# Delta-rule attention and two MoE layers on one core: both row halves in one product, joined grams, anchored filler, later weights

## The chip, the cores and the metric

One core of a Trainium2 chip runs the whole program. The metric is the device time of one execution in microseconds; the median of three runs is given. Smaller is better.

## The reference

For 32 heads of 768 steps, width 48, an attention with a matrix state is computed; its output (3072 tokens of 384) goes through a gated layer and then through a second layer with a leaky nonlinearity:

```python
k_n = k / (norm(k) + 1e-6)
for t in range(S):
    y[:, :, t] = q_t @ state
    state = state + beta_t * outer(k_t, v_t - k_t @ state)
x = ((x @ w_a) * (x @ w_b)) @ w_out
h = x @ w_in
out = (maximum(h, 0) + alpha * minimum(h, 0)) @ w_out2
```

## The kernel before

The 768 steps are cut into 6 superchunks (c) of two steps (j = 0, 1) of 64 positions; in one step 32 pairs of batch and head are worked on, 16 in each row half of the partitions (x = 0, 1). For one superchunk the keys are multiplied with themselves (`g`, the grams of keys, into `ef`) and with the queries (`g` again, into Z[:, 1] and Z[:, 2]); keys lie in Z[:, 0], rows 64 to 111 for one half and 0 to 47 for the other. The 64x64 triangular system of each pair is solved by blocks of 32: `inverting` (line 760) inverts the two diagonal blocks of all pairs at once on VectorE, 31 steps of a multiply into `itmp` and an add into `inv`, a PSUM tile that the code calls `eu`. Then the off-diagonal block is two products, `w` and `xx`; in the first superchunk `first_sides` (861) does them, later ones use `diagonal` and `offdiag`. `w` reads `hw` (the transposed inverse) and `ef`; its result is copied into the upper rows of `hw`; `xx` reads that and `TT`, and its result is copied into `TT`, whose lower column half is a copy of the upper one with zeros above.

`step` (889) then runs for each j: `rp` (old state times keys, not in the very first step), `v` minus it on VectorE, `up` (TT times v) copied to `SU`, `sp` (keys times that) subtracted into the next state, and `yp` (queries times state and `SU`), which is the attention output. `columns` (1108) splits yp into a rounded part on ScalarE and a rest on VectorE, the tile `x` that the first layer reads. That layer streams `p` (two products of x with w_a and w_b, nine instructions of 512 columns each) and `o`, twelve blocks m for each superchunk; the second layer's products are `h` and `o`. Its first superchunk runs from the end of the first attention superchunk on; the second superchunk's attention is interleaved with it.

Weights arrive packed (`raw`), and are decoded by two ScalarE operations, a VectorE shift and a GpSimd add into `W`, then split into `wu` by ScalarE and GpSimd (`decode`, 1020, and `prepare`, 1093). The first four of the twelve have rooms from the start; the later eight use the rooms rawd, rawb, rawc and rawe in turn (1373). `behind` (1039) holds the operation after whose start their transfers are put on SP's queue: the load of the values v of the second superchunk.

The order on each engine is not written by hand. All operations are recorded first; `Schedule.run` (353) then plays them through with a cost for each (`costs`, 277), a level of urgency (`rec.urgent`, added to it) and a model of the product clock, of instruction fetch and of the transfers, and the order that comes out is emitted through one line (203), which is why every row of the profile names L203. An operation recorded on `nc.evict` may go to ScalarE or VectorE, one on `nc.split` to GpSimd or VectorE, as the planner finds it. TensorE's gaps before the first large product are filled with `spin` products of a zero tile `still`: up to 200 are recorded (1238), and the planner puts them into the gaps that it foresees, from the clearing of `still` on:

```python
at = max(free[e], end[warm] if end[warm] else 1e9)
while True:
    each = SPIN if fast(at) else 2 * SPIN
    if at + each > b - REST - 0.08 * (b - free[e]) or len(spins) == len(s.spins):
        break
    spins.append(at)
```

VectorE clears the rooms of two Z and of TT at the start (583, 597). For the second superchunk (N) the grams of keys and of queries are separate products (1290 to 1293), emptied by ScalarE.

## Time and profile before

| | |
|---|---|
| runs | 1018.55 us median of 3 (1017.36 to 1018.96) |
| profiled execution | 1014.57 us, span 1012.8 us |
| TensorE | 996.3 us busy (98% of the span), mean granted clock 0.993 |
| VectorE, ScalarE, GpSimd | 619.2, 459.9 and 486.8 us busy |
| chain that ended last | TensorE 92%, VectorE 5% |
| transfers | 61.41 MB |

The profile is one execution on the chip. A row of the timeline gives a start and a length, merged where an engine repeats the same operation (the count follows the x), then in brackets the idle time of the engine just before and what ended it. TensorE's products have ends that are modelled, so a busy TensorE is not always one at its best. Tiles bear the names that the code gives them: the inverse of the first superchunk is `inv`.

### The profile page before, as it was taken

What the parts mean: (1) busy time and instruction counts of PE and PEld (TensorE: products, weight loads), DVE (VectorE), ACT (ScalarE), POOL (GpSimd) and SP (SyncE); (2) the same over time, 40 slices, a digit from 0 to 9 for tenths busy, and PEclk for the clock granted to TensorE, in tenths of its full rate; (3) what the DMA queues carried; (4) which work ended last, traced back from release to release, by engine and by line L of the source; (5) the groups of instructions that cost most, each with busy time, mean ns of one, the idle gap of its engine ahead of it and who ended that gap; (6) DMA issues with size and microseconds to landing.
All of it is one profiled execution on the core that took longest, in us unless ns stands there. A gap on an engine that the chain in (4) does not pass through costs nothing.

```text
span 1012.8 us, 23700 instructions
## 1 busy us (share of the span) xinstructions
PE 996.3 (98%) x10047; PEld 816.4 (81%) x10047; DVE 619.2 (61%) x1229; ACT 459.9 (45%) x846; POOL 486.8 (48%) x395
## 2 busy tenths in 40 slices
PE   7989999999999999999999999999999999999997
PEld 6777877888888788888878888888888888888886
DVE  7789868846794687568667689343343343433333
ACT  5836785464546454645588786121121221211211
POOL 5467955634653366346456986333333333333332
PEclk8899999999999999999999999999999999999999
DMA  9436433002200220000025542010010020000000
GB/s 236 174 99 226 149 81 94 19 2 66 95 1 22 69 72 1 18 19 32 16 82 173 162 145 84 1 31 32 1 63 1 1 63 1 32 0 1 32 1 32
DMA packets 27083, 61.41 MB, mean 61 GB/s; under 512 B 4320, under 2 KB 8928, under 8 KB 26976
## 3 DMA queue, kind: packets, MB, share of 16 engines
q1 hardware_dynamic: 26544, 59.50, 19.1%
q8 instruction: 79, 1.29, 0.5%
q10 hardware_dynamic: 432, 0.39, 0.1%
q14 instruction: 28, 0.23, 0.1%
HBM read 50.44 MB, written 9.44 MB: 59 GB/s over the span
## 4 chain that ended last, share of the span: by engine, by line
PE 92%; DVE 5%; issue 1%; ACT 1%; DMA 1%; SPq 0%; POOL 0%; DVEq 0%; ACTq 0%
PE o L203 33%; PE p L203 27%; PE h L203 19%; PE g L203 3%; PE spin L203 2%; PE yp L203 2%; PE up L203 2%; DVE inv L203 1%; PE sp L203 1%; DVE itmp L203 1%; PE rp L203 1%; PE xx L203 1%; PE w L203 1%; DMA raw<-in_w_o_dram 1%; DVE a L203 0%
## 5 line engine op out<-in xcount | busy, mean ns | idle before, releaser
L203 PE MATMUL p<-x,wu 128*128 128x512 f32 x1296 | 318.3, 394 | 0.9 <-DVE x L203 0.4
L203 PEld LDWEIGHTS p<-x,wu 128*128 128x128 f32 x1296 | 240.3, 188 | 54.5 <-issue 2.8
L203 POOL TENSOR_TENSOR g<-neg,g 128x512 fp32r<-128x512 f32 x95 | 124.2, 1308 | 259.6 <-ACT g L203 257.1
L203 POOL TENSOR_TENSOR wu<-W,wu 128x768 fp32r<-128x768 f32 (+1 forms) x122 | 175.4, 1442 | 141.6 <-ACT wu L203 141.5
L203 PE MATMUL o<-g,v 128*128 128x512 f32 x870 | 211.4, 388 | 0.0
L203 PE MATMUL h<-x,v 128*128 128x512 f32 x864 | 211.3, 389 | 0.0
L203 DVE TENSOR_SCALAR neg<-h,al 128x512 f32<-128x512 f32 (+1 forms) x97 | 72.2, 745 | 225.6 <-PE h L203 225.6
L203 ACT CAST g<-neg 128x512 fp32r<-128x512 f32 (+1 forms) x97 | 59.7, 616 | 300.5 <-DVE neg L203 278.4
L203 PEld LDWEIGHTS o<-g,v 128*128 128x128 f32 x870 | 162.5, 188 | 33.5 <-POOL g L203 0.2
L203 PEld LDWEIGHTS h<-x,v 128*128 128x128 f32 x864 | 162.2, 188 | 33.7 <-DVE neg L203 0.2
L203 PE MATMUL o<-g,wu 128*128 128x512 f32 x648 | 164.6, 394 | 1.1 <-ACT g L203 1.0
L203 PEld LDWEIGHTS o<-g,wu 128*128 128x128 f32 x648 | 120.1, 188 | 28.0 <-ACT g L203 1.8
L203 ACT CAST wu<-W 128x768 fp32r<-128x768 f32 (+1 forms) x144 | 97.1, 676 | 83.6 <-PE p L203 61.7
L203 POOL TENSOR_TENSOR g<-a,g 128x512 fp32r<-128x512 f32 x50 | 67.7, 1355 | 52.3 <-ACT g L203 51.9
L203 DVE TENSOR_TENSOR inv<-inv,itmp 128x110 f32<-128x110 f32 (+12 forms) x256 | 75.1, 293 | 8.7 <-ACT eu L203 0.4
L203 DVE SCALAR_TENSOR_TENSOR neg<-h,neg 128x512 f32<-128x512 f32 (+1 forms) x97 | 66.5, 686 | 3.3
L203 PE MATMUL g<-Z 48*64 48x64 f32 (+1 forms) x1024 | 63.7, 264 | 4.4 <-issue 2.0
L203 ACT COPY a<-p 128x512 f32<-128x512 f32 x72 | 42.2, 587 | 49.2 <-PE p L203 34.6
L203 DVE TENSOR_TENSOR a<-p,a 128x512 f32<-128x512 f32 x59 | 40.5, 687 | 32.1 <-PE p L203 28.5
L203 PEld LDWEIGHTS g<-Z 48*64 48x64 f32 x1024 | 47.4, 149 | 7.8 <-issue 2.7
L203 DVE TENSOR_TENSOR itmp<-inv,gd 128x96 f32<-128x96 f32 (+8 forms) x150 | 40.7, 271 | 10.5 <-ACT gd L203 6.1
L203 ACT CAST g<-a 128x512 fp32r<-128x512 f32 x59 | 36.5, 619 | 22.7 <-DVE a L203 22.4
(107 smaller groups left out, 950.6 us busy)
## 6 DMA issues: line engine op xcount, KB each, us to landing
v<-in_w_o_dram SPq DMA_DIRECT2D x16, 384.0 KB, 3.4
v<-in_w_in_dram SPq DMA_DIRECT2D x16, 384.0 KB, 3.5
Z<-in_kt_dram SPq DMA_DIRECT2D x24, 192.0 KB, 3.4
Z<-in_qt_dram SPq DMA_DIRECT2D x24, 192.0 KB, 3.8
v<-in_vn_dram SPq DMA_DIRECT2D x12, 384.0 KB, 3.3
x2d<-x2s SPq DMA_DIRECT2D x18, 256.0 KB, 2.3
xf<-x2d SPq DMA_DIRECT2D x18, 256.0 KB, 2.7
raw<-in_w_a_dram SPq DMA_DIRECT2D x11, 384.0 KB, 7.0
```

Of the source, the lines that this page charges most:

```text
L203: getattr(s.engines[op.eng], name)(*(real(x) for x in op.a), **{w: real(x) for w, x in op.k.items()})
```

## The change

1. In `first_sides` w and xx become products over all 128 rows: a tile `both` with zeros holds the two row halves in separate columns, so one product with 64 columns does both. For this `hw` is transposed into TT's lower column half, copied into `both` (ScalarE for one half, GpSimd for the other), and TT's upper half is copied there between w and xx; TT's zeros and the copy of its lower half are written after that, all on GpSimd. Left operands get zeros (`got`, `ef`). w and xx are recorded by j.
2. Keys come in one transfer of 128 rows, padded with zeros on the host, in place of two of 48 rows.
3. The second superchunk's grams of keys and queries are one product with 128 columns (`pair`), emptied by `nc.evict`; so are the copies to SU of the first superchunk, `keep` in `mate`, and one of the first key evictions goes to VectorE.
4. The beta multiply of the first inversion is split between VectorE (8 of 32 columns) and GpSimd; the clears of Z go to GpSimd.
5. Spins come in two sets of 150; the second hangs on a ScalarE operation that reads row 20 of the inverse and writes into `still`.
6. The transfers of the later weights are put behind the last product of the step (`yp`), rawd takes the room of `both`, and in the second step the state update is less urgent than yp. yp of the second step has banks of its own.
7. `rp` runs half by half in the first superchunk, and rp and yp can be cut into pieces (`cut`) between which the planner may put other products. The cost of a transfer goes by its rows.

Left out below are the emission of `neg`, the bookkeeping of the marks, the clears that move and the host's padding.

```diff
@@ -282,7 +287,7 @@
...
-            t.cost, t.lag = 0.42 if t.eng == SP_ else 0.1, 0.05 + n / (9.8e4 if name == "raw" else 6.5e4)
+            t.cost, t.lag = 0.42 if t.eng == SP_ else 0.1, 0.05 + n / (9.8e4 if moved.p[1] - moved.p[0] > 64 else 5.2e4)
@@ -412,17 +417,21 @@
...
-                    at = max(free[e], end[warm] if end[warm] else 1e9)
-                    while True:
+                    first = chunk["at"] == 2 * len(spins)
+                    mark = anchor if end[anchor] else warm
+                    at = max(free[e], end[mark])
+                    while end[mark] and len(spins) < (len(s.spins) if end[anchor] else s.early):
...
-                        if at + each > b - REST - 0.08 * (b - free[e]) or len(spins) == len(s.spins):
+                        if at + each > b - (0 if first else REST if end[anchor] else REST + 0.08 * (b - free[e])):
...
+                        if end[anchor] and len(spins) < s.early:
+                            spins += [None] * (s.early - len(spins))
...
-                        spins.append(None)
+                        spins += [None] * (len(s.spins) + 1 - len(spins))
@@ -622,8 +629,7 @@
...
-            nc.sync.dma_start(Z[64:112, 0], s.kt[c, j, 0])
-            nc.sync.dma_start(Z[0:48, 0], s.kt[c, j, 1])
+            nc.sync.dma_start(Z[:, 0], s.kt[c, j])
@@ -710,7 +716,7 @@
...
-                nc.vector.tensor_scalar(L["ef"][:, j * 16 + i4 : j * 16 + i4 + 4, :], g[:, :, 0, :], -1.0, None, ALU.mult)
+                nc.evict.neg(L["ef"][:, j * 16 + i4 : j * 16 + i4 + 4, :], g[:, :, 0, :])
@@ -723,6 +729,20 @@
...
+    def pair(s, L, j, i4, tag):
+
+        nc, Z = s.nc, L["Z"][j]
+        g = s.bank("g", tag).rearrange("p (i w n) -> p i w n", w=2, n=64)
+        for i in range(4):
+            for x, rows, both in ((0, slice(64, 112), slice(0, 2)), (1, slice(0, 48), slice(0, 3, 2))):
+                nc.tensor.matmul(
+                    g[64 * x : 64 * x + 64, i], Z[rows, 0, i4 + i, :], Z[rows, both, i4 + i, :], start=True, stop=True,
+                )
+        nc.evict.neg(L["ef"][:, j * 16 + i4 : j * 16 + i4 + 4, :], g[:, :, 0, :])
+        for x in range(2):
+            sl = slice(64 * x, 64 * x + 64)
+            nc.evict.neg(Z[sl, 1 + x, i4 : i4 + 4, :], g[sl, :, 1, :])
+
@@ -734,7 +754,7 @@
...
-        s.nc.scalar.activation(L["ef"][:, j * 16 + i8 : j * 16 + i8 + 8, :], g, AF.Copy, scale=-1.0)
+        (s.nc.vector if L.get("first") and j and i8 else s.nc.scalar).neg(L["ef"][:, j * 16 + i8 : j * 16 + i8 + 8, :], g)
@@ -766,13 +786,14 @@
...
-        nc.vector.tensor_tensor(a0[:, :, 0:8], a0[:, :, 0:8], bt[:, :, 0:8], ALU.mult)
-        nc.vector.tensor_tensor(a0[:, :, 8:32], a0[:, :, 8:32], bt[:, :, 8:32], ALU.mult)
+        bt = L["bt"].unsqueeze(1).to_broadcast([128, 32, 32])
+        for eng, ms in ((nc.vector, slice(0, 8)), (nc.gpsimd, slice(8, 32))):
+            eng.tensor_tensor(a0[:, ms], a0[:, ms], bt[:, ms], ALU.mult)
...
-            column = a0[:, k:32, m : m + 1].to_broadcast([128, nt, k])
+            column = a0[:, m, k:32].unsqueeze(2).to_broadcast([128, nt, k])
@@ -858,33 +879,54 @@
...
-    def first_sides(s, L):
-
-        nc, ef, hw, eu = s.nc, L["ef"], s.ap.tile([128, 32, 32], F32, tag="mb", name="hw", bufs=1), L["eu"]
+    def first_sides(s, L, both):
+
+        nc, ef, eu = s.nc, L["ef"], L["eu"]
+        got = s.ap.tile([128, 32, 32], F32, tag="mb", name="hw", bufs=1)
...
+        cols = (slice(0, 32), slice(32, 64))
+        urgent, s.nc.urgent = s.nc.urgent, 0.0
+        nc.gpsimd.memset(got, 0.0)
+        nc.gpsimd.memset(both, 0.0)
+        for x in range(2):
+            nc.gpsimd.memset(ef[high[x], :, 32:64], 0.0)
+        s.nc.urgent = urgent
+        hw = TT[:, :, 0:32]
...
+        for j in range(2):
+            js = slice(16 * j, 16 * j + 16)
+            for x in range(2):
+                (nc.gpsimd.tensor_copy if x else nc.scalar.copy)(both[low[x], js, cols[x]], hw[low[x], js])
...
-        for j in range(2):
-            for sl in low:
-                nc.gpsimd.tensor_copy(TT[sl, 16 * j : 16 * j + 16, 0:32], TT[sl, 16 * j : 16 * j + 16, 32:64])
-        stages = (
-            (low, ef[:, :, 32:64], hw, high, hw, [s.bank("w") for _ in range(2)]),
-            (high, hw, TT[:, :, 32:64], low, TT[:, :, 32:64], [s.bank("xx", "ab") for _ in range(2)]),
-        )
-        for here, left, right, there, to, banks in stages:
+
+        def side(left, there, to, bank):
+            bank = bank.rearrange("p (i n) -> p i n", n=64)
...
-                        for x in range(2):
-                            nc.tensor.matmul(
-                                banks[x][32 * q : 32 * q + 32, 32 * i : 32 * i + 32],
-                                left[here[x], 8 * q + i, :], right[here[x], 8 * q + i, :], start=True, stop=True,
-                            )
+                        nc.tensor.matmul(
+                            bank[32 * q : 32 * q + 32, i], left[:, 8 * q + i, :], both[:, 8 * q + i, :], start=True, stop=True,
+                        )
+                yield
...
-                        got = banks[x][32 * q : 32 * q + 32, 0:256].rearrange("p (i n) -> p i n", n=32)
-                        (nc.vector if x else nc.scalar).copy(to[there[x], 8 * q : 8 * q + 8, :], got)
+                        (nc.vector if x else nc.scalar).copy(to[there[x], 8 * q : 8 * q + 8, :], bank[32 * q : 32 * q + 32, :, cols[x]])
+
+        w = side(ef[:, :, 32:64], high, got, s.bank("w"))
+        next(w)
+        for j in range(2):
+            js = slice(16 * j, 16 * j + 16)
+            for _ in zip(range(1), w):
+                pass
+            for x in range(2):
+                (nc.gpsimd.tensor_copy if x else nc.scalar.copy)(both[high[x], js, cols[x]], TT[high[x], js, 32:64])
+        for sl in low:
+            nc.gpsimd.tensor_copy(TT[sl, :, 0:32], TT[sl, :, 32:64])
+        for sl in high:
+            nc.gpsimd.memset(TT[sl, :, 0:32], 0.0)
+        for _ in side(got, low, TT[:, :, 32:64], s.bank("xx", "ab")):
+            pass
@@ -910,12 +952,15 @@
...
-            for i in range(8):
-                for h, (o, _) in enumerate(halves):
-                    near, far = slice(64 * h, 64 * h + 64), slice(64 - 64 * h, 128 - 64 * h)
-                    nc.tensor.matmul(rp[h][near, i, :], Z[64:112, 0, o + i, :], SU[0][64:112, o + i, 0:48], start=True, stop=True)
-                    nc.tensor.matmul(rp[h][far, i, :], Z[0:48, 0, o + i, :], SU[1][0:48, o + i, 0:48], start=True, stop=True)
-                beside(i)
+            for i, h in [(i, h) for i in range(8) for h in range(2)] if c else [(i, h) for h in range(2) for i in range(8)]:
+                o = halves[h][0]
+                s.nc.now_tag = "cut" if i == 0 and not c else None
+                near, far = slice(64 * h, 64 * h + 64), slice(64 - 64 * h, 128 - 64 * h)
+                nc.tensor.matmul(rp[h][near, i, :], Z[64:112, 0, o + i, :], SU[0][64:112, o + i, 0:48], start=True, stop=True)
+                s.nc.now_tag = None
+                nc.tensor.matmul(rp[h][far, i, :], Z[0:48, 0, o + i, :], SU[1][0:48, o + i, 0:48], start=True, stop=True)
+                if h:
+                    beside(i)
@@ -938,7 +983,7 @@
...
-                    (nc.scalar if c or not x else nc.vector).copy(SU[x][64 * x : 64 * x + 64, hs, 0:48], ups[n][at : at + 64])
+                    (nc.scalar if c else nc.evict).copy(SU[x][64 * x : 64 * x + 64, hs, 0:48], ups[n][at : at + 64])
@@ -964,11 +1009,16 @@
...
-        yp = [s.bank("yp", tag) for _ in range(2)]
+        if st == 1:
+            yp = s.pools["g"].tile([128, 2, 512], F32, tag="inv", name="yp")
+            yp = [yp[:, n] for n in range(2)]
+        else:
+            yp = [s.bank("yp", tag) for _ in range(2)]
...
+                s.nc.now_tag = None if c else "cut"
@@ -978,6 +1028,7 @@
...
+                        s.nc.now_tag = None
@@ -1232,12 +1283,18 @@
...
+        rec.now_tag = "mark"
...
-        rec.now_tag, spin = "spin", A.bank("spin", "g")
-        for _ in range(200):
-            nc.tensor.matmul(spin, still[:, 0:128], still, start=True, stop=True)
-        rec.now_tag = None
+        spin = A.bank("spin", "g")
+
+        def spinning(n):
+            rec.now_tag = "spin"
+            for _ in range(n):
+                nc.tensor.matmul(spin, still[:, 0:128], still, start=True, stop=True)
+            rec.now_tag = None
+
+        spinning(150)
@@ -1270,7 +1327,7 @@
...
-        rawa, rawb, rawd = triple(wp, "w6"), triple(wp, "w7"), triple(xp, "x1")
+        rawa, rawb = triple(wp, "w6"), triple(wp, "w7")
@@ -1279,7 +1336,7 @@
...
-                A.fold(L, j, nc.gpsimd.tensor_copy)
+                A.fold(L, j, nc.vector.tensor_copy if j else nc.gpsimd.tensor_copy)
@@ -1287,15 +1344,16 @@
...
-        for n, (j, i8) in enumerate(HALF):
-            A.keep_keys(N, j, i8, A.gram_keys(N, j, i8, ("chain", "pre")[n % 2]))
-        for n, (j, i8) in enumerate(HALF):
-            A.keep_queries(N, j, i8, A.gram_queries(N, j, i8, ("chain", "pre")[n % 2]))
+        for n, (j, i4) in enumerate((j, i4) for j in range(2) for i4 in range(0, 16, 4)):
+            A.pair(N, j, i4, ("chain", "pre", "chain")[n % 3])
...
+        rec.now_tag = "mark"
+        nc.scalar.mul(still[:, 0:8], L["eu"][:, 20, 0:8], 0.0)
+        spinning(150)
@@ -1350,7 +1408,7 @@
...
-        A.first_sides(L)
+        A.first_sides(L, xp.tile([128, 32, 64], F32, tag="x1", name="both"))
@@ -1360,14 +1418,17 @@
...
-                    behind[:] = [A.load_values(1, N)]
+                    A.load_values(1, N)
+                    rec.urgent = URGENT * (j == 0)
+                if (i, j) == (5, 1):
...
+            behind[:] = [rec.ops[-1]]
...
-        rawc = triple(wp, "w8")
+        rawc, rawd = triple(wp, "w8"), triple(xp, "x1")
```

## Rows read from the trace of the kernel before

**Rows 1.** Stretches: busy time (and instructions) of each engine, granted clock, transfers

```profile
0.00:74.80 74.80, 65.28 (x1442) 54.14 (x1442) 60.54 (x133) 45.16 (x80) 40.47 (x55) 0.91 0.58 166
...
180.00:1012.80 832.80, 827.10 (x7220) 679.76 (x7218) 471.85 (x897) 342.76 (x646) 375.79 (x293) 1.00 0.13 41
```

**Rows 2.** Timeline of the start: start, length, engine, operation

```profile
0.80 1.83 POOL L203 MEMSET Z<- 32x1024 f32 x2 [0.29 <-POOLq L1587]
...
2.84 0.91 DVE L203 MEMSET Z<- 32x1024 f32 x1 [0.25 <-issue]
...
7.07 1.82 DVE L203 TENSOR_REDUCE ss<-sq 128x16 f32<-128x768 f32 x2
...
9.74 1.94 PEld L203 LDWEIGHTS g<-Z 48*64 48x64 f32 x62 [0.23 <-DMA Z<-in_kt_dram]
...
13.89 1.97 DVE L203 STREAM_TRANSPOSE eu<-ef 128x1024 f32<-128x1024 f32 x1 [2.37 <-POOL ef L203]
...
15.90 1.29 DVE L203 TENSOR_TENSOR eu<-eu,bt 128x256 f32<-128x256 f32 x2
...
17.11 0.19 DVE L203 TENSOR_TENSOR itmp<-inv,eu 128x31 f32<-128x31 f32 x1
...
30.29 1.47 POOL L203 TENSOR_TENSOR v<-v,m 128x768 f32<-128x768 f32 x1
```

**Rows 3.** Timeline, the end of the inversion and w

```profile
39.18 8.46 PE L203 MATMUL spin<-still 128*128 128x512 f32 x36
...
40.65 2.16 DVE L203 STREAM_TRANSPOSE hw<-inv 128x1024 f32<-128x1024 f32 x1
...
44.77 2.59 POOL L203 COPY TT<-TT 32x512 f32<-32x512 f32 x4 [3.44 <-DVE TT L203]
...
47.57 1.29 PE L203 MATMUL w<-hw,ef 32*32 32x32 f32 x128
```

**Rows 4.** Timeline, the two steps of the first superchunk

```profile
54.71 1.65 PE L203 MATMUL up<-v,TT 64*64 64x48 f32 x49 [1.06 <-issue]
...
57.26 1.03 DVE L203 COPY SU<-up 64x384 f32<-64x384 f32 x2
...
59.69 2.00 PE L203 MATMUL yp<-Z,SU 112*32 112x64 f32 x128
...
65.28 1.69 DVE L203 TENSOR_TENSOR v<-rp,v 128x384 f32<-128x384 f32 x3
```

**Rows 5.** Timeline, from the second yp to the first large product

```profile
69.02 1.31 SPq L203 DMA_DIRECT2D raw<-in_w_a_dram  x1
...
69.91 2.06 PE L203 MATMUL yp<-Z,SU 112*32 112x64 f32 x128
...
71.89 0.92 ACT L203 CAST x<-yp 128x256 fp32r<-128x256 f32 x3 [1.48 <-PE yp L203]
...
73.88 1.09 DVE L203 TENSOR_TENSOR x<-yp,x 128x256 fp32r<-128x256 f32 x3
...
74.78 4.35 PE L203 MATMUL p<-x,wu 128*128 128x512 f32 x18 [0.36 <-DVE x L203]
...
77.62 1.24 ACT L203 ACTIVATE W<-raw 128x1152 int32<-128x1152 uint32 x1 [4.81 <-DMA raw<-in_w_o_dram]
```

**Rows 6.** Stretches: the inversion, then up to the second one's start and end

```profile
17.11:40.62 23.51, 22.37 (x329) 19.07 (x329) 21.41 (x63) 16.60 (x27) 11.41 (x15) 0.71 0.85 294
...
40.62:70.89 30.27, 27.04 (x795) 22.12 (x798) 23.43 (x38) 17.47 (x34) 15.21 (x16) 1.00 0.13 34
...
70.89:118.60 47.71, 47.06 (x300) 37.79 (x289) 44.09 (x118) 30.96 (x44) 38.32 (x23) 1.00 0.64 209
```

**Rows 7.** Timeline, the end of the second superchunk's attention

```profile
157.08 0.96 ACT L203 COPY SU<-up 64x384 f32<-64x384 f32 x2 [0.25 <-PE up L203]
...
164.92 2.00 PE L203 MATMUL yp<-Z,SU 112*32 112x64 f32 x128
...
169.03 4.24 PE L203 MATMUL p<-x,wu 128*128 128x512 f32 x18
```

More of the change, by code (lines that the diff above doesn't have):

```diff
@@ L249, in __init__ @@
         s.spins = [op for op in rec.ops if op.tag == "spin"]
+        s.marks = [op for op in rec.ops if op.tag == "mark"]
+        s.early = sum(op.n < s.marks[1].n for op in s.spins)
         for op in rec.ops:
@@ L253, in __init__ @@
             t = s.tasks[-1] if s.tasks else None
-            if op.eng == PE_ and not large(op) and t and t.eng == PE_ and not t.large and t.ops[-1].n == op.n - 1:
+            if op.eng == PE_ and not large(op) and t and t.eng == PE_ and not t.large and t.ops[-1].n == op.n - 1 and op.tag != "cut":
                 t.ops.append(op)
@@ L363, in run @@
         clock = {"w": 0, "fast": False}
-        warm = s.of[min(s.spins[0].before)]
+        warm, anchor = (s.of[x.n] for x in s.marks)
         def fast(b):
@@ L1542, in columns, with stacked @@
         return a.reshape(NSC, 2, 2, D, 16, 64)
+    def stacked(a):
+        a = columns(a)
+        gap = np.zeros((NSC, 2, 16, 16, 64), a.dtype)
+        return np.concatenate([a[:, :, 1], gap, a[:, :, 0], gap], 2)
     def rows(a):
```

13 lines of the change are left out of this document (7 added, 6 removed).

## The prediction

> **What bounds the kernel now.** I read the stretches first. From the first large product to the end TensorE is nearly full: from 180 us on it is busy 827.10 of 832.80 us [rows 1]. Nothing in the change touches those products, so what it can give lies in the opening stretch, 74.8 us long, in which TensorE's 65.28 busy us are largely filler products on a tile of zeros (the "spins") and small products that wait for other engines. The forecast is therefore the answer to one question: how much earlier does the first large product (p, at 74.78 us) begin, and how much of that do the next 100 us keep?
>
> Second, the timeline of the start. VectorE clears rooms, sums squares from 7.07 us, transposes at 13.89 us after a wait of 2.37 us for GpSimd's fold, multiplies by beta for 1.29 us and begins the triangular inversion at 17.11 us [rows 2]. That inversion is one chain on one engine until 40.6 us, when its result is transposed into hw (40.65 plus 2.16, so 42.81 us). Now the first surprise: w, which needs only hw and old data, starts at 47.57 us, because TensorE works off 36 spins from 39.18 to 47.64 us [rows 3]. The order of every engine is written out ahead by a planner; between 17.11 and 40.62 us TensorE was granted a mean clock of 0.71, so a good part of that stretch ran at the 1.2 GHz level [rows 6], it came out behind the planner's clock, and the spins that were to fill a gap now stand in front of w.
>
> Third, the line from w to p: one product kind after another, each with a copy between [rows 4], and at its end p waits for VectorE's last splits of x at 73.88 us although ScalarE had its own done at 72.81 us [rows 5].
>
> **The change, part by part.** All sums are in the profiled execution (1014.57 us, span 1012.8 us and 1.8 us around it). It lies 4.0 us under the median of the runs shown; I take the difference off the median.
>
> (A) Start of the inversion. The beta multiply was 1024 elements in 1.29 us on VectorE; now GpSimd does 768 of them. VectorE keeps a quarter of the elements, with its fixed part some 0.4 us, so 0.9 us go. GpSimd's nearest row, 768 elements, takes 1.47 us [rows 2]; its columns are first read in the ninth of 31 steps, which lies about 4 us in (31 steps take 23.5 us), so the cover is wide; without it 1.1 us would come back. Four clears of 0.91 us leave VectorE (two for Z go to GpSimd at 0.92 each, two for TT go later): the sums at 7.07 us can begin when the squares are there. The fourth key eviction and one fold move to VectorE, so that GpSimd's fold no longer ends last. The keys come as one transfer of 512 KB for each j in place of two of 192 KB; the last landed at 9.74 us. No row has that form: if bytes rule it lands half a us later, if the number of transfers rules 1.5 us earlier. Together these three are worth between -0.5 and 2.4 us (the wait on the fold); with late keys as likely as early ones I take the middle, 1.2. Part A: 2.1 (0.4 to 3.3).
>
> (B) The spins. 42.81 to 47.57 is 4.76 us of pure delay. In the new kernel the second set of spins hangs on a ScalarE operation that reads row 20 of the inversion, so the planner's error counts only from there on, not from the start. Against it, w now needs hw copied into a tile with zeros: one 32x512 copy for each row half, GpSimd's row gives 0.65 (2.59 for four) [rows 3], and with hand-overs I count 1.25. Part B: 3.5 (0 if the spins end as late as now; 3.9 at best).
>
> (C) w and xx. From w to the end of the first up is 47.57 to 56.36, 8.79 us [rows 3, 4]. Each of w and xx becomes 32 products over all 128 rows with 64 columns in place of 64 products of 32 rows with 32 columns. The nearest row is yp: 64 products of 112 rows and 64 columns in 2.00 us, so 32 in 1.0 against 1.29 now, 0.6 saved on both. Between w and xx there is a new copy of TT into the tile (0.65, ScalarE and GpSimd beside each other), since that room is read by w first. The longest line is GpSimd's: four copies of 0.65, the two TT copies that were 2.59 as four, and two clears of 0.92 that were at the start [rows 2, 3], together 7.0 us in order from 42.81, and up reads all of it. So up begins about 7.5 us after hw and ends some 2 us later, against 13.55 now; with the 4.76 less 1.25 of part B this leaves 0.5. Pipelining w and xx by j adds a little: I take 0.8 (-3 if the copies line up one behind another, 3 if GpSimd's line is not the last).
>
> *A rule against this part.* w as 64 tiled products takes 1.29 us, and yp, which already runs over 112 rows, is no slower for each product [rows 3, 4]. The Trainium skill (TensorEngine Tiling (Array Packing), When to Use Tiling) says that a contraction of 32 rows should take fourfold row tiling, which is what the change gives up: four tiles in place of sixteen, half as many products, twice the columns, so up to four times the time. By it the sum would lose twice 3.9 us. yp's row speaks for my value.
>
> (D) The two steps, end of the first up (56.36) to the end of the second yp (71.97): 15.61 us. Three losses are visible [rows 4]: the SU copies wait for VectorE until 57.26 (0.9; now either engine may take them); the first yp, 2.00 us, stands between sp and rp (now it may be cut and passed); v is subtracted from 65.28 on, 3.6 us after yp ends, where rp needs about 1.1 and a hand-over (some 2 lost to other VectorE work, and that work stays). 4.9 at most, nothing at least; about half, 2.5, since VectorE has the same work in less time.
>
> (E) yp to p, 71.97 to 74.78. The second yp gets banks of its own, so p no longer waits for VectorE to empty two banks (73.88 plus 1.09), only for ScalarE's three casts, done at 72.81 [rows 5]. That is 2.0; the last products of the first nine still need VectorE's part 1.4 us later. I take 1.5 (0 to 2.4).
>
> Sum: 2.1 + 3.5 + 0.8 + 2.5 + 1.5 = 10.4 us, p at about 64.4.
>
> (F) What is given back. The weights after the fourth are now sent behind the second yp and not behind the last load of v: 69.02 us is 5.8 before p, the new place about 3.0, so they land 2.8 later against p. ScalarE already stood 4.81 us before the first of them (77.62) with a<-p queued behind it [rows 5], and TensorE's next p waits for that copy: 0.7 (0 to 2.8). VectorE is idle 6.84 us between 40.62 and 70.89 and 3.62 us up to 118.60 [rows 6]: the second inversion can come forward by A and most of the 6.84, some 8 us, so 2.4 less than p. The second superchunk has room for it: its last SU is done at 158.04 and yp issues at 164.92, 6.9 us later, with p at 169.03 [rows 7]. I count 0.5 (0 to 3). The padded keys add 128 KB a transfer in stretches where no row shows an engine waiting for keys: 0, up to 0.5. The joined grams of the second superchunk halve TensorE's products there; spins fill whatever that frees, so 0, as long as the evictions (24 small ones for 12) stay off VectorE's inversion. Net 10.4 - 1.2 = **9.2 us**: 1018.55 - 9.2 = 1009.3.
>
> **Rivals.**
> 1. *VectorE becomes the bound (0.14).* p moves but the second inversion does not, the second superchunk's x is late, TensorE stands near 165 us, and only A and some idle time count: 4 us, 1014.5. For it: 44.09 busy of 47.71 us [rows 6]. Against: the 6.9 us of room [rows 7].
> 2. *The 128-row products are slow (0.04).* If w and xx cost four times their rows, twice 3.9 us go: 9.2 - 7.8 = 1.4, 1017.1. yp's row speaks against it [rows 4]; this is the tiling rule of the Trainium skill's page named above.
> 3. *Most terms near their upper ends (0.12).* 15 us, 1003.5.
> 4. *The change doesn't do what it says (0.06).* All orders come from one planner whose transfer costs changed too. A new plan may put other work in each gap: 1018.5.
> 5. *Slower: transfers too late (0.14).* One room (rawd) takes four of the eight late weights, each after the last was decoded, and it now starts behind the tile of the first sides. If in each of the four turns ScalarE's wait grows by those 2.8 us and all of that, with the 0.7 of today's, reaches TensorE through the a<-p behind it, 14 us go against a gain of 9.9 (9.2 and the 0.7 already taken off): 4.1 slower, 1022.7. It decides as soon as the wait at 77.62 grows beyond 7 us in every turn. Against: today's wait costs TensorE under 1 us.
>
> **How the numbers follow.** The forecast (6 to 13 us, 1005.5 to 1012.5) has 0.50. Faster takes the forecast, rivals 1 and 3, and a third of rival 2: 0.77. Same (within 0.2%, about 2 us, which is what a measurement of this kernel can tell from no change) takes the rest of 2 and rival 4: 0.09. Slower is rival 5: 0.14. The range reaches from all terms at their upper ends (17 us, rounded to 1002) to no change at all (1018.5), and leaves out rival 5 and the tail of 3, under 2 in 10.
>
> **What would show it.** Right: the inversion begins near 15.0; w within 2 us of hw; up about 8 us after hw; p starting on ScalarE's x, near 64; after that stretches as full as before. Wrong: spins still in front of w (B), GpSimd's line of copies ending long before up or far later (C), p still on VectorE's x (E), or idle time of TensorE between p and 180 us with raw transfers or DVE as releaser (F, rivals 1 and 5).

## The result, and the profile after

The changed kernel takes 1025.05 us (median of 4 runs, 1023.73 to 1025.96) against 1018.75 us before: ratio 1.0063, 95% interval 1.0046 to 1.0081. It is slower by more than the 0.2% that can be told from no change; the forecast was 1009.3 us.

The profiled execution took 1023.73 us (span 1021.7). It lies 1.3 us under its median and that of before 4.2 under its own, so the two traces are 9.2 us apart where the medians are 6.3 apart. The stretches answer to [rows 1, 6]: the time up to p, the inversion, from its end to the start of the second superchunk's, and from there to the transpose of the second hw. Columns: busy us (and instructions) of PE, PEld, DVE, ACT, POOL; granted clock, DMA share, GB/s.

```profile
0.00:74.52 74.52, 62.09 (x1126) 51.89 (x1127) 53.01 (x116) 48.38 (x98) 47.17 (x61) 0.88 0.58 175
16.38:45.66 29.28, 27.16 (x264) 23.15 (x264) 21.41 (x62) 22.08 (x45) 16.32 (x25) 0.77 0.73 241
45.66:75.78 30.12, 25.00 (x692) 20.83 (x691) 23.56 (x39) 18.40 (x40) 18.86 (x20) 0.92 0.27 88
75.78:120.92 45.14, 44.57 (x218) 35.84 (x218) 40.22 (x110) 30.78 (x43) 37.95 (x22) 0.98 0.57 184
...
180.00:1021.70 841.70, 835.24 (x7251) 686.11 (x7250) 465.65 (x881) 357.52 (x678) 391.72 (x307) 1.00 0.14 42
```

The inversion takes the same 21.41 us of VectorE's work as before, but 29.28 us of time instead of 23.51. From 180 us on TensorE is as full as before and has 8.1 us more to do: what was not worked off earlier is left over. The stretch from 75 to 180 us shows where, first before, then after:

```profile
75.00:180.00 105.00, 103.68 (x1388) 82.28 (x1388) 86.67 (x200) 72.00 (x121) 70.36 (x48) 1.00 0.45 140
```

```profile
75.00:180.00 105.00, 100.42 (x1388) 79.33 (x1388) 82.38 (x185) 70.37 (x122) 68.32 (x46) 0.97 0.43 136
```

TensorE is idle 3.3 us more, and by the mean clock of 0.97 some 3 us of its 100 are lost to the lower level (an estimate from that row).

The opening, on VectorE (start, length, engine, line, operation, idle time before and its releaser): the inversion starts 0.7 us earlier than in [rows 2], and then stands still in its twenty-first step (m = 20).

```profile
15.92 0.43 DVE L206 TENSOR_TENSOR eu<-eu,bt 128x256 f32<-128x256 f32 x1
16.38 0.19 DVE L206 TENSOR_TENSOR itmp<-inv,eu 128x31 f32<-128x31 f32 x1
...
38.45 0.41 DVE L206 TENSOR_TENSOR inv<-inv,itmp 128x231 f32<-128x231 f32 x1 [5.73 <-ACT still L206]
```

The releaser is the ScalarE operation that starts the second set of spins. It reads row 20 of inv, so VectorE's next write to inv waits for it, and on ScalarE it stands behind the next superchunk's evictions:

```profile
36.01 1.26 ACT L206 ACTIVATE Z<-g 64x256 f32<-64x256 f32 x3
37.30 0.93 ACT L206 ACTIVATE W<-raw 128x768 int32<-128x768 uint32 x1
38.24 0.18 ACT L206 ACTIVATE still<-inv 128x8 fp32r<-128x8 f32 x1
```

TensorE from there to p, answering to [rows 3 to 5]:

```profile
38.48 8.48 PE L206 MATMUL spin<-still 128*128 128x512 f32 x36 [0.55 <-ACT still L206]
49.28 2.28 PE L206 MATMUL w<-both,ef 128*32 128x64 f32 x64 [2.33 <-ACT both L206]
...
56.20 2.36 PE L206 MATMUL up<-v,TT 64*64 64x48 f32 x64
...
69.37 1.81 PE L206 MATMUL yp<-Z,SU 112*32 112x64 f32 x113 [0.17 <-issue]
71.11 0.56 PE L206 MATMUL sp<-SU,k 64*48 64x48 f32 x15
73.92 0.67 PE L206 MATMUL sp<-SU,k 64*48 64x48 f32 x17 [2.25 <-issue]
74.52 7.89 PE L206 MATMUL p<-x,wu 128*128 128x512 f32 x27
```

w starts 1.7 us later than before, p 0.3 us earlier. From p to the end of the span it is 947.2 us instead of 938.0, so 9.2 us are lost after p. The 0.3 us is not firm: the trace of before lies 4.2 us under its median, and in four runs below whose TensorE order up to the second yp is that of the kernel before (f4, h2, k1, k2) p starts at 77.2 to 80.0 us. Two places on VectorE stand out. The second superchunk's inversion starts at 75.78 us instead of 70.89 [rows 6], behind most of what the first superchunk still had queued:

```profile
72.49 1.08 DVE L206 TENSOR_TENSOR x<-yp,x 128x256 fp32r<-128x256 f32 x3
73.48 0.54 DVE L206 TENSOR_SCALAR raw<-raw 128x384 int32<-128x384 int32 x1
74.63 1.12 DVE L206 TENSOR_TENSOR SU<-SU,sp 48x384 f32<-48x384 f32 x2 [0.60 <-PE sp L206]
75.78 0.20 DVE L206 TENSOR_TENSOR itmp<-inv,gd 128x30 f32<-128x30 f32 x1
```

And at its end two state updates (SU) of the first superchunk, left over, come between its two transposes. Before, then after:

```profile
119.11 2.29 DVE L203 STREAM_TRANSPOSE hw<-eu 128x1024 f32<-128x1024 f32 x1
121.28 2.08 DVE L203 STREAM_TRANSPOSE TT<-eu 128x1024 f32<-128x1024 f32 x1
```

```profile
120.92 2.17 DVE L206 STREAM_TRANSPOSE hw<-eu 128x1024 f32<-128x1024 f32 x1
123.12 1.12 DVE L206 TENSOR_TENSOR SU<-SU,sp 48x384 f32<-48x384 f32 x2
124.27 0.69 DVE L206 TENSOR_TENSOR g<-p,g 128x512 fp32r<-128x512 f32 x1
124.88 2.03 DVE L206 STREAM_TRANSPOSE TT<-eu 128x1024 f32<-128x1024 f32 x1
```

TensorE waits for that SU in the middle of w, and nine p behind it take 3.86 us (granted clock 0.56 from 125.60 to 129.40 us) where nine take 2.23 before:

```profile
123.24 0.22 PE L206 MATMUL w<-hw,ef 32*32 32x32 f32 x2 [1.15 <-DVE hw L206]
124.39 1.28 PE L206 MATMUL w<-hw,ef 32*32 32x32 f32 x126 [0.93 <-DVE SU L206]
125.60 3.86 PE L206 MATMUL p<-x,wu 128*128 128x512 f32 x9
```

```profile
82.55 2.23 PE L203 MATMUL p<-x,wu 128*128 128x512 f32 x9
```

The second superchunk's rp follows at 136.44 us; before it was 132.13.

### The profile page after: what moved, and what is told of

It reads as the page before. It is cut to its first block, busy times and chain, and to the rows that moved or that the text cites. A ratio compares the mean times of both kernels' runs of the same rounds, so it can differ in the third digit from the quotient of the medians.

```text
span 1021.7 us, 23161 instructions
## 1 busy us (share of the span) xinstructions
PE 998.2 (98%) x9764; PEld 817.8 (80%) x9764; DVE 601.4 (59%) x1181; ACT 476.3 (47%) x897; POOL 507.7 (50%) x414
## 4 chain that ended last, share of the span: by engine, by line
PE 90%; ACT 3%; DMA 2%; POOL 2%; DVE 1%; issue 1%; SPq 0%; DVEq 0%; POOLq 0%; ACTq 0%
PE o L206 32%; PE p L206 27%; PE h L206 19%; PE g L206 3%; PE yp L206 2%; PE up L206 2%; PE sp L206 1%; PE rp L206 1%; DMA Z<-in_qt_dram 1%; POOL W L206 1%; PE w L206 1%; PE xx L206 1%; ACT W L206 1%; DMA raw<-in_w_b_dram 1%; ACT raw L206 0%
## 5 line engine op out<-in xcount | busy, mean ns | idle before, releaser
L206 POOL TENSOR_TENSOR wu<-W,wu 128x384 fp32r<-128x384 f32 (+1 forms) x125 | 176.2, 1414 | 125.9 <-ACT wu L206 120.2
L206 POOL TENSOR_TENSOR g<-a,g 128x512 fp32r<-128x512 f32 x56 | 77.0, 1375 | 62.8 <-ACT g L206 62.6
L206 PE MATMUL g<-Z 48*64 48x128 f32 (+1 forms) x896 | 63.7, 279 | 5.8 <-DMA Z<-in_kt_dram 1.9
L206 DVE TENSOR_TENSOR Z<-g,mask 64x256 f32<-64x256 f32 x64 | 27.0, 422 | 23.7 <-PE g L206 15.9
```

The source lines that it names most:

```text
L206: getattr(s.engines[op.eng], name)(*a, **k)
```

## The experiments

Ratios are to the kernel before, run on the same chip. Theories 1 and 2 are those of the first four runs: the anchor (the ScalarE operation above) is the main loss; or the loss is made after p.

**e1, the anchor on VectorE**, reading into a second zero tile:

```diff
-        nc.scalar.mul(still[:, 0:8], L["eu"][:, 20, 0:8], 0.0)
-        spinning(150)
+        rec.urgent = 20 * URGENT
+        nc.vector.tensor_scalar(still2[:, 0:8], L["eu"][:, 20, 0:8], 0.0, None, ALU.mult)
+        spinning(150, still2)
```

> The changed kernel with the anchor of the second spins moved from ScalarE to VectorE, where it stands in order behind the step that makes row 20 final, and writes into a second zero tile of its own. Theory 1 (the wait of 5.73 us of VectorE for ScalarE's anchor is the main loss): no wait in the inversion, which ends near 40 instead of 45.7 us; p begins near 69 instead of 74.5; 1019.3 us (1017 to 1021), ratio to the kernel before near 1.000. Theory 2 (the loss is made after p, by late transfers, half clock and the second superchunk): p begins near 69 too, but the second superchunk's x comes as late as now and the time stays above 1023.

Measured: 1.0034 (1.0015 to 1.0053). The wait is gone, but w starts only at 51.62 us, behind 37 spins that now ran at the lower clock and took 10.82 us. This interval and that of 1.0063 overlap, so no gain is shown.

**e2, one set of spins, no anchor**, in the changed kernel (the planner's spin code as before):

```diff
-        spinning(150)
+        spinning(200)
...
-        nc.scalar.mul(still[:, 0:8], L["eu"][:, 20, 0:8], 0.0)
-        spinning(150)
```

> The changed kernel with the spins of the kernel before: one set, no anchor. Theory 1: VectorE's wait is gone, the inversion ends near 40 us, but w stands behind some 33 spins again and starts near 46; p near 71, 1021 us. Theory 2: above 1023.

Measured: 1.0064 (1.0037 to 1.0091): nothing gained. TensorE stands 3.61 us before w and does w, xx and up at the lower clock (mean 0.69 from 40 to 60 us).

**e3, the anchor alone on the kernel before** (with the change's spin code in the planner):

```diff
-        for _ in range(200):
+        spinning(150)
...
+        nc.scalar.mul(still[:, 0:8], L["eu"][:, 20, 0:8], 0.0)
+        spinning(150)
```

> The kernel before with the two sets of spins and ScalarE's anchor, nothing else of the change. Theory 1: VectorE waits in the middle of the inversion for ScalarE, by as much as ScalarE is behind the planner's clock, 3 to 6 us; w comes after it without a long row of spins; 1018 to 1023 us, so no gain from the anchor. Theory 2: no wait, or a harmless one; w up to 4 us earlier, 1015 to 1017.

Measured: 1.0038 (1.0019 to 1.0058). VectorE waits 1.06 us, w is 3.7 us earlier at 43.88, and the next products give it back at the lower clock (up 3.64 us). p starts at 74.81 us, as before; the loss of this execution lies behind it (943.0 us from p to the end, against 938.0).

**e6, e1 with the transfers and the urgency of the second step as before:**

```diff
-                    A.load_values(1, N)
-                    rec.urgent = URGENT * (j == 0)
+                    behind[:] = [A.load_values(1, N)]
+                    rec.urgent = URGENT
...
-            behind[:] = [rec.ops[-1]]
```

> As the first one, and with the later weight transfers and the urgency of the second step's state update put back to what they were in the kernel before. If late transfers and the late state update cost what the trace suggests between p and the second superchunk (2 to 4 us), this is 2 to 4 us faster than the first one, about 1016; if they cost nothing, equal to it within 1 us.

Measured: 1.0025 (1.0003 to 1.0047), not to be told from e1. Its p starts at 71.99 us, 2.8 earlier than before, and the profiled execution is 3.3 us longer (1017.89): **the start of p does not set the end.** Neither theory explains that, so the parts were tried alone, each added to the kernel before; theory 2 was narrowed to the supply of weights by GpSimd and VectorE.

**f1, the start** (stacked keys, Z's clears, eu's product, last eviction and fold):

```diff
-            nc.sync.dma_start(Z[64:112, 0], s.kt[c, j, 0])
-            nc.sync.dma_start(Z[0:48, 0], s.kt[c, j, 1])
+            nc.sync.dma_start(Z[:, 0], s.kt[c, j])
...
+        for eng, ms in ((nc.vector, slice(0, 8)), (nc.gpsimd, slice(8, 32))):
+            eng.tensor_tensor(a0[:, ms], a0[:, ms], bt[:, ms], ALU.mult)
```

> The kernel before with the start of the inversion alone changed (keys stacked in one transfer, Z's memsets on GpSimd, the last fold and the last key eviction on VectorE, the 768-wide product of eu on GpSimd, eu read along rows). Theory 1 (what the start gains is kept, and the anchor and the spins lose it again): the inversion starts 1 to 2 us earlier and the time falls by 1 to 2 us, ratio 0.998 to 0.999. Theory 2 (the weight conversions on GpSimd and VectorE between 50 and 135 us set the time, and GpSimd gets work here in every superchunk): the inversion starts earlier all the same, but the time stays within 0.2% of before or is up to 2 us longer, ratio 1.000 to 1.002.

Measured: 0.9985 (0.9963 to 1.0008), not to be told from no change. Its inversion starts at 17.08 us, no earlier than before, which neither theory expected.

**f2, w and xx in one product** (the new first_sides, TT's clear at the start left out, rawd allocated late):

```diff
-        A.first_sides(L)
+        A.first_sides(L, xp.tile([128, 32, 64], F32, tag="x1", name="both"))
...
-        rawc = triple(wp, "w8")
+        rawc, rawd = triple(wp, "w8"), triple(xp, "x1")
```

> The kernel before with only w and xx of the first superchunk changed (both row halves in one product, with the copies and memsets on GpSimd that this needs, and with the raw buffer that gives up its place to them). Theory 1: w to the end of the first up is about equal or 0.8 us shorter, and the time is that of before or 1 us less, ratio 0.999 to 1.000. Theory 2: GpSimd's work of 7 us in front of its first weight addition moves all its conversions back, the fourth addition (a 128x1152) ends after 72.4 us, the product loop waits for GpSimd's wu or for VectorE between 100 and 135 us, and the time is 2 to 3 us longer, ratio 1.002 to 1.003.

Measured: **1.0069** (1.0037 to 1.01). w starts at 47.30 us and the first yp at 60.02, as before (47.57, 59.69), so the products themselves are not what costs it; p starts at 77.27, and p to the end takes 946.1 us. VectorE's line afterwards, with bt's line of before in front:

```profile
63.32 0.20 DVE L203 STREAM_TRANSPOSE bt<-b 128x32 f32<-128x32 f32 x1
```

```profile
68.40 0.56 DVE L203 COPY SU<-up 64x384 f32<-64x384 f32 x1 [1.40 <-ACT SU L203]
...
71.00 0.56 DVE L203 COPY SU<-up 64x384 f32<-64x384 f32 x1 [1.58 <-ACT SU L203]
...
72.05 2.35 DVE L203 TENSOR_TENSOR SU<-SU,sp 48x384 f32<-48x384 f32 x4
74.43 0.21 DVE L203 STREAM_TRANSPOSE bt<-b 128x32 f32<-128x32 f32 x1
...
77.83 0.19 DVE L203 TENSOR_TENSOR itmp<-inv,gd 128x30 f32<-128x30 f32 x1
```

bt, the first input of the second inversion, is transposed at 74.43 us although b was ready at 65.06; before it was at 63.32. In the written order it stands behind copies that wait for ScalarE's half of SU, which waits for TensorE's up (2.51 and 2.13 us, at 67.90 and 70.50). The inversion starts 6.9 us later than before.

**f3, the grams in pairs** (and the negated evictions of the later superchunks free to go to ScalarE):

```diff
-            A.keep_keys(N, j, i8, A.gram_keys(N, j, i8, ("chain", "pre")[n % 2]))
...
+            A.pair(N, j, i4, ("chain", "pre", "chain")[n % 3])
```

> The kernel before with the next grams taken with keys beside queries, and with the negated eviction of these and of the later superchunks' grams free to go to ScalarE. Theory 1: nothing measurable, ratio 0.999 to 1.001. Theory 2: ScalarE gets evictions of every later superchunk in place of VectorE; if VectorE is the tight one between 75 and 135 us this gives back up to 1 us, ratio 0.999 to 1.000; if ScalarE's share of the conversions is late instead, 1 to 2 us longer.

Measured: 0.9968 (0.9944 to 0.9993), a gain that neither theory gave in full; p starts at 71.95, the second inversion at 68.06 us.

**f4, later transfers and the lowered urgency** (rawd late as in f2):

```diff
-                    behind[:] = [A.load_values(1, N)]
-                    rec.urgent = URGENT
+                    A.load_values(1, N)
+                    rec.urgent = URGENT * (j == 0)
...
+            behind[:] = [rec.ops[-1]]
```

> The kernel before with only the later weight transfers (values and raw weights let go at the end of the step instead of at its third piece, rawd allocated later, the urgency of the second step lowered). Theory 1: a part that costs nothing, since the loss sits at the anchor and at the half clock before the first products: ratio 0.999 to 1.001. Theory 2: the conversions that these transfers feed come later, TensorE idles or waits for wu, hw or o's operands between 100 and 180 us, and the time is 1.5 to 3 us longer, ratio 1.0015 to 1.003.

Measured: 1.0040 (1.0012 to 1.0067), and the same wait of w for SU (0.91 us) as in the changed kernel.

This gave theory 3: the place of the second inversion in VectorE's order.

**h1, its head first in the changed kernel** (finish(norms), the folds of N and inverting_halves up to the gd copies):

```diff
+        rec.urgent = 500.0
         finish(norms)
...
+                rec.urgent = 500.0
                 A.inverting_halves(N, "pre")
```

> The changed kernel, with one thing added: the norms, folds and first operations of the second superchunk's inversion get a priority that puts them ahead of the first superchunk's last steps in VectorE's, ScalarE's and GpSimd's order. Theory 3 (the second superchunk's inversion, queued on VectorE behind the first superchunk's last steps, starts at 75.8 us in the changed kernel against 70.9 before; VectorE is busy without a gap from there to the transpose of hw, and so its start sets the time): it starts 3 to 6 us earlier than 75.8, though the first products may start 1 to 2 us later, and the time falls by 3 to 6 us against the changed kernel, ratio to before 1.000 to 1.003. Theory 2 (weights and GpSimd): no gain, or a loss by the later first products, ratio 1.006 to 1.008.

Measured: 1.0048 (1.0023 to 1.0074). The inversion starts at 71.91 us, but hw's transpose at 119.97 is only 1.0 earlier and rp no earlier (136.66): three SU now stand between the transposes, and w waits 0.85 us for them. Theory 3 alone falls short.

**h2, the head late in the kernel before** (first: its first step on VectorE; columned: the evictions of x):

```diff
                 A.inverting_halves(N, "pre")
+                for x in columned:
+                    first.before[x.n] = 1
```

> The kernel before, with the first step of the second superchunk's inversion ordered behind the last eviction of x in VectorE's order, and nothing else held back. Theory 3: the inversion starts at about 75 us instead of 70.9, the transpose of hw and w of the second superchunk come 3 to 4 us later, and the time is 3 to 6 us longer, ratio 1.003 to 1.006. If the start is only a sign of a late queue and VectorE makes up for it by doing its other work first, the time is that of before, ratio 0.999 to 1.001.

Measured: 1.0026 (1.0004 to 1.0049), between the two expectations; the inversion starts at 78.31, 0.8 us behind p instead of 3.9 ahead of it.

**g1, three parts together:** f1's and f3's edits and those of the steps:

```diff
-            for i in range(8):
-                for h, (o, _) in enumerate(halves):
+            for i, h in [(i, h) for i in range(8) for h in range(2)] if c else [(i, h) for h in range(2) for i in range(8)]:
...
+        if st == 1:
+            yp = s.pools["g"].tile([128, 2, 512], F32, tag="inv", name="yp")
```

> The kernel before with three parts of the change: the start of the inversion, the next grams in pairs, and the two steps with freer evictions; without the second set of spins, without w and xx in one product, without the later transfers. If the parts add up: the start -0.15% and the pairs -0.3% by their own runs, the steps 0 to -0.3%, ratio 0.993 to 0.996. By theory 3 the second inversion starts at 68 us or earlier; if it starts later than 71 us, the ratio is 1.000 or above whatever the first products do.

Measured: **0.9965** (0.994 to 0.999), faster than both kernels. p starts at 65.48 us, 9.3 earlier than before, and the profiled execution is 2.4 us shorter. The other 6.9 us are given back after p: TensorE is idle 4.9 us between 75 and 180 us, against 1.3 before. The two longest gaps are waits for weights, the third (1.12 us, at 116.64) is w's wait for the second inversion, which starts 2.7 us behind p:

```profile
102.62 1.66 PE L206 MATMUL o<-g,wu 128*128 128x512 f32 x6 [1.29 <-POOL wu L206]
114.53 0.98 PE L206 MATMUL o<-g,wu 128*128 128x512 f32 x3 [1.24 <-DVE wu L206]
```

**g2, the old w and xx in the changed kernel** (the old first_sides, TT cleared at the start):

```diff
-        A.first_sides(L, xp.tile([128, 32, 64], F32, tag="x1", name="both"))
+        A.first_sides(L)
```

> The changed kernel with the old w and xx of the first superchunk (32-row products and GpSimd's four copies), all else of the change kept. If the parts add up: that part alone cost 0.69% on the kernel before, so the ratio falls from 1.0063 to 0.999 to 1.001. If the anchor's wait of 5.7 us and the late second inversion stay, it falls by half of that or less, ratio 1.003 to 1.006, and the second inversion still starts after 73 us.

Measured: 1.0001 (0.9979 to 1.0024). Taken out, the part gives back what it costs when added (f2). p starts at 68.92 us, 5.9 earlier than before, and nothing of that is left: the second inversion starts at 71.09, behind p, and TensorE is idle 7.0 us between 75 and 180 us.

**k1 and k2 split f4.** k1 is f4 with

```diff
-                    rec.urgent = URGENT * (j == 0)
+                    rec.urgent = URGENT
```

and k2 the kernel before with

```diff
-                    rec.urgent = URGENT
+                    rec.urgent = URGENT * (j == 0)
+                if (i, j) == (5, 1):
+                    rec.urgent = URGENT
```

> The kernel before with the later transfers alone (values and raw weights held back until the step's last eviction, one raw buffer allocated after the steps), the second step's urgency as before. With both, the ratio was 1.0040, and from hw's transpose to rp of the second superchunk 15.6 us passed instead of 13.0. If the transfers cause it: ratio 1.003 to 1.004, and the 15.6 us stay. If the lowered urgency causes it (w waits 0.91 us for VectorE's state update, which holds its bank): ratio 0.999 to 1.001, and the stretch is 13 us.

> The kernel before with the lowered urgency of the second step's last pieces alone, the transfers as before. If the urgency causes it: VectorE's state update of the second step comes next to the transpose of hw at about 120 us, w waits for it, TensorE falls to its lower clock behind it, ratio 1.002 to 1.004. If the transfers cause it: ratio 0.999 to 1.001.

Measured: k1 1.0010 (0.9984 to 1.0035), k2 1.0030 (1.0008 to 1.0053). The intervals overlap, so the times alone do not split f4; the rows speak for the urgency. k2 alone has the SU between the transposes:

```profile
122.41 2.24 DVE L203 STREAM_TRANSPOSE hw<-eu 128x1024 f32<-128x1024 f32 x1
124.68 1.12 DVE L203 TENSOR_TENSOR SU<-SU,sp 48x384 f32<-48x384 f32 x2
```

```profile
125.85 1.27 PE L203 MATMUL w<-hw,ef 32*32 32x32 f32 x126 [0.91 <-DVE SU L203]
...
132.30 1.91 PE L203 MATMUL xx<-TT,hw 32*32 32x32 f32 x128 [2.23 <-ACT hw L203]
```

In k1 the two transposes follow each other (121.83, 123.99) and w does not wait, though its stretch from hw to rp stayed long (14.6 us).

**k3, f2 with the head first** (h1's edit, on f2):

> The kernel before with w and xx in one product (ratio 1.0069 alone; second inversion from 77.8 us), and the norms, folds and first operations of the second inversion put ahead. If the late second inversion is what w and xx in one product cost: it starts at 70 to 73 us and the ratio falls to 1.001 to 1.004. If that start is only a sign of how much work VectorE has left at 75 us: it starts earlier, hw's transpose comes no more than 1 us earlier than 124.6, and the ratio stays at 1.005 to 1.008.

Measured: **1.0000** (0.9984 to 1.0017), from 1.0069. Neither expectation fits whole. The head, put ahead, first holds up the first inversion, since the clearing of the second one's tile stands in it and waits for ScalarE:

```profile
37.94 0.48 DVE L203 MEMSET inv<- 128x512 f32 x1 [5.58 <-ACT Z L203]
```

So w comes late (51.03 us), and p at 78.98. The second inversion starts at 75.08, only 2.8 us earlier than in f2, and hw's transpose comes no earlier at all (124.58 against 124.59). What is as before again is its place against p: 3.9 us ahead, where f2 has it 0.6 behind. TensorE does 104.00 us in the stretch from 75 to 180 us, f2 100.89:

```profile
75.00:180.00 105.00, 104.00 (x1489) 82.36 (x1478) 85.80 (x197) 70.45 (x120) 67.17 (x46) 1.00 0.46 144
```

```profile
75.00:180.00 105.00, 100.89 (x1369) 79.17 (x1358) 84.20 (x188) 69.25 (x119) 66.42 (x46) 0.97 0.43 136
```

Both wait for the same chain from hw to rp; k3 has products to fill the time with, f2 has not, and behind its gap the lower clock is granted (0.66 from 135 to 145 us, 1.00 in k3). k3, then f2:

```profile
137.67 1.18 PE L203 MATMUL rp<-SU,Z 48*64 48x48 f32 x64
```

```profile
136.85 2.33 PE L203 MATMUL rp<-SU,Z 48*64 48x48 f32 x64 [1.96 <-ACT TT L203]
```

**k4, f2 with GpSimd's copies and clears after the transposes on VectorE:**

```diff
-                (nc.gpsimd.tensor_copy if x else nc.scalar.copy)(both[low[x], js, cols[x]], hw[low[x], js])
+                (nc.vector.tensor_copy if x else nc.scalar.copy)(both[low[x], js, cols[x]], hw[low[x], js])
...
-            nc.gpsimd.memset(TT[sl, :, 0:32], 0.0)
+            nc.vector.memset(TT[sl, :, 0:32], 0.0)
```

> The kernel before with w and xx in one product, and the copies and memsets that follow the transposes on VectorE instead of GpSimd. If GpSimd's 7 us in front of its weight additions are what it costs: the additions come 3 to 5 us earlier and the ratio falls from 1.0069 to 1.002 to 1.004. If VectorE's remaining work at 75 us is what counts: no gain, ratio 1.006 to 1.009.

Measured: 1.0075 (1.0049 to 1.01). It tells less than was meant: GpSimd's first weight addition came at 60.02 us, later than f2's 53.32, so its load was not tested by itself.

**l1 and l2, the whole change with its orders put right.** l1 is the changed kernel with h1's edit and

```diff
-                    rec.urgent = URGENT * (j == 0)
+                    rec.urgent = URGENT
```

l2 has e1's anchor besides.

> The changed kernel, all its parts kept, with two priorities changed: the second superchunk's norms, folds and first operations ahead, and the second step's urgency not lowered. If the loss is one of order, made by these two and by the anchor: against 1.0063, head first takes back 0.0065 (as it did on w and xx in one product alone) and the urgency 0.003 (as it cost alone), so the ratio is 0.997 to 1.000 with the anchor's wait still in it. If the parts' own work costs the time: 1.003 or more.

> The same, and the anchor of the second set of spins on VectorE, reading into a second zero tile, so that VectorE's own steps don't wait for ScalarE. If the loss is one of order: another 0.003 less, ratio 0.994 to 0.998, so that all parts of the change together are faster than the kernel before. If the parts' own work costs the time: 1.000 or more.

Measured: l1 **1.0007** (0.9983 to 1.0032), l2 1.0009 (0.9985 to 1.0033). Two priorities take back the loss, with every part kept. l1's two transposes follow each other again, although its inversion still waits for the anchor (3.26 us); without that wait l2 is no faster. The gain that l2's expectation hoped for did not come.

**Side by side**, the twenty traces show what goes with the loss after p. Where the second inversion starts 3.9 us or more ahead of p (before, f1, f3, f4, k1, k2, k3), p to the end of the span takes 937.9 to 939.6 us, and 942.4 in k2. Where it starts 2.4 to 3.2 ahead (e3, l1, l2), that takes 941.7 to 943.0, and 947.9 in h1 with its three SU between the transposes. Where it starts behind p (the changed kernel, e1, e2, e6, f2, g1, g2, h2, k4), it takes 943.5 to 947.7. So neither start counts by itself, but the one against the other. h2 and k3 set out to move that place; in the others it moved along with the rest, one execution each.

## Why the prediction was wrong, point by point

**(A)** 2.1 forecast, 0.7 found (16.38 against 17.11 us). The products and clears shrank as counted (multiply 0.43 instead of 1.29), but the fold of the last keys, now on VectorE, ends at 13.7 us and the transpose begins at 13.98, no earlier than in [rows 2]. The 0.7 does not stand for the part: in the ten traces with the new start the inversion begins at 15.06 (g1) to 18.78 us (e6), in the middle at 17.1, and in the ten with the old one at 16.91 to 17.11. The forecast's 2.1 came in g1 alone.

**(B)** "the planner's error counts only from there on" holds: from hw's transpose to w it is about 1.6 us instead of 4.76. What the step left out is the other side of the anchor: it reads a tile that VectorE writes, and "hangs on a ScalarE operation" means that VectorE's chain waits for ScalarE's queue. That was 5.73 us, more than the 3.5 forecast as gain. No row for the queue in front of it was read. So (B) failed too, but it does not decide: with the wait gone, e2 took as long as the changed kernel, and for e1 no gain is shown.

**(C)** 0.8 forecast, 0.5 lost (49.28 to 58.56, 9.28 us against 8.79). w's 32 products (64 records) took 1.79 us at the full clock in f2 where yp's row gave 1.0. That yp "is no slower for each product" is misread: 64 products in 2.00 us are 31 ns each, w's in 1.29 us 20. Nor is yp's row the same case: its products go round four column groups (q from 0 to 3), the new w's round two; whether that makes the difference no run shows. The Trainium skill (TensorEngine Tiling (Array Packing), When to Use Tiling) says that a contraction of 32 rows should take fourfold row tiling. The run agrees in direction: 1.79 against 1.29 us is 1.4 times. It does not test the fourfold, since the old products stood in two of the four row groups (eight tiles, not the prediction's sixteen).

**(D)** 2.5 forecast, 3.0 found (58.56 to 71.18, 12.62 us against 15.61). The mechanism is right (rp now stands in front of yp, at 62.03 and 64.58 us); part of it is sp moved behind yp.

**(E)** 1.5 forecast, 0.5 lost (71.18 to 74.52). p no longer waits for x, but half of sp stands in between, and TensorE stalled 2.25 us inside it, for nothing that the profile shows.

**(F) is the step that failed.** It let 1.2 us of the gain at p be given back. From p to the end the traces show 9.2 us more than before; in g1 p moved by 9.3 and 6.9 of it were given back, in g2 it moved by 5.9 and nothing was left. The sum took "how much earlier does the first large product" begin for the question, but TensorE has other products to fill with from p to 180 us. What counts there, by the traces side by side, is how far the second inversion is when p starts; g1's rows show the weights beside it. (F) let the second inversion "come forward by A and most of the 6.84"; it went back 4.9, from 3.9 us ahead of p to 1.3 behind it, because its order was read as a consequence of free time and not looked up as a place in a queue. The runs show two such places. One is its head behind the first superchunk's steps: moving its first step alone cost 0.26% on the kernel before (h2), and putting it ahead took f2 from 1.0069 to 1.0000 (k3), though not by an earlier end of the inversion. The other is the lowered urgency of the second step, which stands in the diff and has no term in the sum: 0.30% in k2, with the SU between the transposes. With both put right the whole change goes from 1.0063 to 1.0007 (l1). The transfers, on which (F) and rival 5 stood, are not shown to cost anything: k1 is 1.0010 with an interval up to 1.0035, ScalarE's wait before the first late weight is 4.39 us there, 4.81 in [rows 5], and in the changed kernel its first late weight (79.26 us) shows no wait.

**Rivals.** Rival 1 (VectorE as the bound) came nearest, but was priced as a smaller gain; its own case, a second inversion that comes later, was missing, and TensorE's gaps lie at 112 to 153 us, not near 165. Rival 4 held in part: a part that saves its own time moved others in the plan.

**Left open.** The start, pairs and steps gain 0.35% together (g1), the whole change with its orders put right nothing (l1); which of the second spins, w and xx, and the transfers takes that 0.4% was not separated. The anchor costs 0.38% on the kernel before (e3) and nothing measurable in l1 against l2; why is not shown. The head first was not run on the kernel before, nor the urgency alone in the changed kernel, so how the 0.56% that l1 takes back divides between the two is open; head first alone (h1) is not to be told from the changed kernel.

## What to carry to other kernels

When the order of every engine is written ahead, an edit is priced by what it puts behind what: look up, on each queue that it touches, the next chain's first operation and what stands in front of it. An earlier start of the big engine is worth only as much as its suppliers are ahead; measure how far they are when it starts (here the second inversion's start against p), not the first big product. An operation that only reads a tile held up the tile's writer here (5.73, 3.26 and 1.06 us), so a marker read from a slow queue belongs on the writer's own engine or behind its last write; the first took the wait away in e1, but no run shows time gained by it, and the second was not tried.

## What was not expected of the hardware

An idle gap before a run of small products cost twice in e2: after 3.61 us of idle time w took 2.48 us, xx's first half 2.21 and up 3.72, against 1.79, 1.35 and 2.14 in f2, where spins had filled most of that gap; the granted clock of 40 to 60 us was 0.69 there and 1.00 in f2. The same lower level was granted behind the 2.25 us stall before p in the changed kernel: the first 27 p took 7.89 us (granted clock 0.79 from 74.52 to 82.30 us) where 18 before took 4.35.
